# The softmax of q in the second to fourth block: two of its steps on GpSimd in place of VectorE

## Chip, cores and metric

The kernel runs on one core of a Trainium2 chip. The metric is the device time of one execution in microseconds (us), lower is better. The engines are named as in the profile: PE is TensorE's matrix products and PEld its weight loads, DVE is VectorE, ACT is ScalarE, POOL is GpSimd, SP is SyncE. A trailing q (SPq, DVEq) means an engine's sequencer.

## The reference

All in float32, cut to what matters:

```
# q, k, v: (4 batches, 8 heads, 576 tokens, 64)
q_s = softmax of q over its last axis (64 numbers of one token and head)
k_s = softmax of k over the tokens
kv  = k_s^T v                      # 64 x 64 for each batch and head
x   = q_s kv                       # -> 2304 tokens x 512
h   = x w1_in;  x = (h - tanh(h)) w1_out     # 512 -> 2048 -> 512
h   = x w2_in;  out = softplus(h) w2_out     # 512 -> 2048 -> 512
```

The softmax of q is q minus its maximum, the exponential, and a division by the sum plus 1e-9.

## The kernel before

The 2304 tokens are cut into five blocks of 512, 256, 512, 512 and 512 (SIZES; block index i counts from 0). For each block the attention output, transposed, is made by four tasks `x_task` (one for each pair of heads, hp), and the keys and values of a batch become the 128 x 128 matrices kv by four tasks `kv_task`. The first perceptron then runs in 16 steps over slices of its hidden layer: `hidden` makes h (L364), `gate` takes it through tanh on ScalarE, a subtraction on VectorE (L374, which reads h from PSUM), and a split into a high and a low part (L375 on ScalarE, L376 on VectorE), and `mid_out` (L391 to L393) multiplies by the second weight and adds up in PSUM. Each product is made of three, of high and low parts, to keep precision. Block sums go to memory, and the second perceptron runs over three spans of tokens with a scheme of seven products in place of eight (L459 onward); its last products are L529 to L531.

The weights need work first. They arrive as 64-bit numbers, and `convert` (L123 to L127, alternating between ScalarE and VectorE) makes them into 32-bit ones; `parts` (L132, L133) splits them. The second perceptron's input weights are added up in pairs (L212 to L215), split (L225, L226) and written to memory as `forms` (L227) while the first perceptron runs on blocks with index 2 and 3. All loads and stores stand in SyncE's queue: weights (L104, L109), k and v (L247), q (L311), forms.

An `x_task` has five stages with a pause between them: load q (L311); maximum over 64 columns (L320), subtraction (L322), exponential on ScalarE (L323); sum (L326), plus 1e-9 (L327), reciprocal (L328), normalisation into qn (L330); four transposes on PE (L339) and a copy (L341); product with kv (L346) and a split (L348, L349). The tasks of block i + 1 are started in the steps 1, 4, 8 and 10 of block i, and the `kv_task`s of the next batch in steps 0, 3, 6 and 9. These tasks have one buffer for each tile (q, qn, k, v and so on), so a load of q waits until the qn of the task before is made, and a qn waits for the transposes of the one before. The first block's tasks are interleaved by hand in a string (`order`) and have four buffers.

In a `kv_task`, GpSimd sets the extra columns of the tile v to 1 (L264), VectorE takes a maximum over the tokens of a partition (L268 to L270, tile m), PE transposes it (pm, L273), VectorE reduces it (L275), PE sends it back (pb, L278), VectorE subtracts it, reading it from PSUM (L280), ScalarE takes the exponential (L281), and PE multiplies with v (pk, L285). The normalised result goes into kv on ScalarE (L291).

The order of instructions on each engine is settled when the program is built: a scheduler goes through them by priority (the order in which they are written) and by its own estimate of when each is ready. On the chip each engine then runs its list in order.

The two steps in question run on the engine `eng`, which is GpSimd for the first block and VectorE for the others.

Of the kernel before, what the change touches and what calls it, by code (L numbers as in the profile page):

```python
# [19 lines left out]
def linear_attention_two_mlps(  # L20
# [28 lines left out]
    nc = tc.nc  # L49
# [5 lines left out]
    NB = len(SIZES)  # L55
# [25 lines left out]
    def psum_a(name):  # L81

        tag = wide.pop() if wide else "a"
        return ps.tile([P, 512], F32, tag=tag, name=name, bufs={"acc": 4, "a": 2}.get(tag, 1))
# [4 lines left out]
    def f32(ap):  # L89
        return ap.bitcast(F32)  # L90
# [209 lines left out]
    def x_task(i, hp, pool, bufs):  # L300

        nm = f"{i}_{hp}"
        n, J = SIZES[i], JS[i]
        qt = pool.tile([P, 2, J, D], F32, tag="q", name=f"q{nm}", bufs=bufs)
        segs = []
        r0 = 0
        while r0 < n:
            b, s = divmod(BASE[i] + r0, S)
            rows = min(n - r0, S - s)
            segs.append((b, slice(r0 // J, (r0 + rows) // J)))  # L310
            nc.sync.dma_start(  # L311
                out=qt[r0 // J : (r0 + rows) // J].rearrange("p h j d -> p h (j d)"),
                in_=q[b, 2 * hp : 2 * hp + 2, s : s + rows].rearrange("h (p j) d -> p h (j d)", j=J),
            )
            r0 += rows
        yield
        G = 2 * J
        qg = qt.rearrange("p h j d -> p (h j) d")
        mx = pool.tile([P, G], F32, tag="qm", name=f"qm{nm}", bufs=bufs)
        nc.vector.tensor_reduce(mx, qg, axis=AX, op=ALU.max)  # L320
        eng = nc.vector if i > 0 else nc.gpsimd
        eng.tensor_tensor(qg, qg, mx.unsqueeze(2).to_broadcast([P, G, D]), op=ALU.subtract)  # L322
        nc.scalar.activation(qt, qt, AF.Exp)  # L323
        yield
        sm = pool.tile([P, G], F32, tag="qsum", name=f"qsum{nm}", bufs=bufs)
        nc.vector.tensor_reduce(sm, qg, axis=AX, op=ALU.add)  # L326
        nc.vector.tensor_scalar(sm, sm, 1e-9, None, op0=ALU.add)  # L327
        nc.vector.reciprocal(sm, sm)  # L328
        qn = pool.tile([P, J, 2, D], F32, tag="qn", name=f"qn{nm}", bufs=bufs)
        eng.tensor_tensor(  # L330
            qn.rearrange("p j h d -> p h j d"),
            qt,
            sm.rearrange("p (h j) -> p h j", h=2).unsqueeze(3).to_broadcast([P, 2, J, D]),
            op=ALU.mult,
        )
        yield
        pt = psum_a(f"pt{nm}")
        for j in range(J):
            nc.tensor.transpose(pt[:, j * P : (j + 1) * P], qn[:, j].rearrange("p h d -> p (h d)"), ident)  # L339
        qs = pool.tile([P, n], F32, tag="qs", name=f"qs{nm}", bufs=bufs)  # L340
        nc.scalar.copy(qs, pt[:, :n])  # L341
        yield
        px = psum_a(f"px{nm}")
        pv, qv = (t.rearrange("p (j t) -> p j t", j=J) for t in (px[:, :n], qs))
        for b, c in segs:
            nc.tensor.matmul(pv[:, :, c], kv[b % 2, hp], qv[:, :, c], start=True, stop=True)  # L346
        xh, xl = (t[:, hp, :n] for t in xt[i])
        nc.scalar.activation(xh, px[:, :n], AF.Copy, scale=1.0 / WS)  # L348
        nc.vector.scalar_tensor_tensor(xl, px[:, :n], 1.0 / WS, f32(xh), op0=ALU.mult, op1=ALU.subtract)  # L349
# [216 lines left out]
    for i in range(NB - 1):  # L566
        for hp in range(NHP):
            if i < B - 1:
                at(i, KV_AT[hp], lambda i=i, hp=hp: kv_task(i + 1, hp, att, 1))
            at(i, X_AT[hp], lambda i=i, hp=hp: x_task(i + 1, hp, att, 1))  # L570
# [13 lines left out]
    wide += ["h0", "acc", "a", "acc", "h1", "acc", "a", "acc"] * 2 + ["h0", "acc", "a", "acc"]  # L584
    tasks = {f"k{hp}": kv_task(0, hp, pro, NHP) for hp in range(NHP)}
    tasks |= {f"x{hp}": x_task(0, hp, pro, NHP) for hp in range(NHP)}
    tasks["w"] = w_task(0)
    order = """k0 k1 k2 k3 x0 x1 x2 x3 k0 k0 k1 k1 w k2 k3 k2 k3 x1 k0 x0 k1 k0 x0 w x2 k2 x2 x3 x1 x3 k3 k1 x0 k2 x1 k3 x2 x3 x0 w x2 x3 w x1"""
# [13 lines left out]
    for n in range(min(starts), NB * NF - 2):  # L602
# [6 lines left out]
        while n >= -2 and len(gated) < min(n + 3, len(steps)):  # L609
            i, f = steps[len(gated)]  # L610
            gate(i, f, hidden(i, f, len(gated)))
            gated.append((i, f))
        if n >= 0:
            i, f = steps[n]
# [112 lines left out]
```

## Time and profile before

| | |
|---|---|
| median of 3 runs | 862.87 us (861.86 to 865.49) |
| the profiled execution | 860.99 us, of which 859.2 us lie between its first and last instruction (the span) |
| PE busy | 833.6 us, 97% of the span |
| DVE busy | 537.8 us, 63% |
| ACT busy | 409.3 us, 48% |
| POOL busy | 26.5 us, 3% (44 instructions) |
| chain that ended last | PE 83%, DVE 5%, ACT 5%, DMA 5%, issue 1% |
| mean granted TensorE clock | 0.996 of full speed |

Times in the trace count from the first instruction. A busy share is an average over stages with different limits: VectorE is at nine tenths or more in the first quarter of the span and far lower after it. PE counts as busy while a product is in its pipeline, so a busy PE is not a PE at its peak.

### The profile page before, as it was taken

How to read it: one execution, taken by the hardware profiler on the slowest of the kernel's cores; microseconds unless marked ns; L12 is line 12 of the kernel's file. 1: busy time of each engine (PE TensorE's matmuls, PEld its weight loads, DVE VectorE, ACT ScalarE, POOL GpSimd, SP SyncE). 2: the span in 40 equal slices, each digit the busy share in tenths (PEclk: the TensorE clock that was granted, in tenths of full speed). 3: DMA queues.
4: the chain of work that ended last, by engine and by line, in shares of the span. 5: the costliest groups of instructions: out<-in, count | busy, mean ns of one | idle time of the engine just before them, and what ended most of it. 6: DMA issues, size and time to landing. Idle time of an engine off the chain costs nothing.

```text
span 859.2 us, 11330 instructions
## 1 busy us (share of the span) xinstructions
PE 833.6 (97%) x4152; PEld 718.4 (84%) x4152; DVE 537.8 (63%) x926; ACT 409.3 (48%) x677; POOL 26.5 (3%) x44
## 2 busy tenths in 40 slices
PE   4899999999999999999999999999999999999997
PEld 4578789998787888878888889898899898998996
DVE  7899999998887534334797543357643454634433
ACT  4888666665655323223675442344432343423322
POOL 4000000000000000001011000001000010000000
PEclk9999999999999999999999999999999999999999
DMA  9798117667765010003544644446644444544411
GB/s 261 241 280 276 35 35 235 189 205 234 234 224 175 13 50 12 13 2 122 183 162 157 196 116 121 119 111 198 189 118 121 112 121 119 188 123 112 120 51 74
DMA packets 98616, 121.33 MB, mean 141 GB/s; under 512 B 38657, under 2 KB 62977, under 8 KB 98561
## 3 DMA queue, kind: packets, MB, share of 16 engines
q1 hardware_dynamic: 98560, 120.61, 46.4%
q8 instruction: 33, 0.54, 0.3%
q14 instruction: 23, 0.18, 0.1%
HBM read 96.47 MB, written 24.12 MB: 140 GB/s over the span
## 4 chain that ended last, share of the span: by engine, by line
PE 83%; DVE 5%; ACT 5%; DMA 5%; issue 1%; SPq 0%; ACTq 0%; DVEq 0%
PE h L364 18%; PE one L459 11%; PE o L530 8%; PE o L531 8%; PE o L529 8%; PE x L391 6%; PE x L393 6%; PE x L392 6%; PE seven L459 6%; PE two L459 3%; DMA rawi<-in_moe_w_in_dram 2%; PE px L346 2%; PE pk L285 1%; DMA forms<-stage 1%; DMA rawo<-in_moe_w_out_dram 1%
## 5 line engine op out<-in xcount | busy, mean ns | idle before, releaser
L364 PE MATMUL h<-xh,i 128*128 128x512 f32 (+1 forms) x640 | 202.2, 379 | 1.3 <-DVE i L133 0.7
L364 PEld LDWEIGHTS h<-xh,i 128*128 128x128 f32 x640 | 117.9, 189 | 24.3 <-DVE i L133 1.7
L364 PE MATMUL h<-xl,i 128*128 128x512 f32 (+1 forms) x320 | 118.8, 371 | 0.0
L392 PE MATMUL x<-gl,o 128*128 128x512 f32 (+1 forms) x320 | 118.6, 371 | 0.0
L393 PE MATMUL x<-gh,o 128*128 128x512 f32 (+1 forms) x320 | 118.4, 370 | 0.0
L459 PE MATMUL one<-xf,wf 128*128 128x384 f32 x576 | 116.7, 337 | 0.1
L391 PE MATMUL x<-gh,o 128*128 128x512 f32 (+1 forms) x320 | 116.2, 372 | 0.5 <-ACT gh L375 0.5
L530 PE MATMUL o<-o,gh 128*128 128x512 f32 x288 | 113.7, 395 | 0.0
L531 PE MATMUL o<-o,gh 128*128 128x512 f32 x288 | 113.7, 395 | 0.0
L529 PE MATMUL o<-o,gl 128*128 128x512 f32 x288 | 112.3, 390 | 0.0
L459 PEld LDWEIGHTS one<-xf,wf 128*128 128x128 f32 x576 | 103.0, 188 | 6.6 <-ACT u L474 0.4
L474 ACT COPY u<-one 128x384 f32<-128x384 f32 x72 | 34.5, 479 | 108.0 <-PE one L459 108.0
L374 DVE TENSOR_TENSOR g<-h,g 128x512 f32<-128x512 f32 (+1 forms) x80 | 50.5, 632 | 54.2 <-ACT g L373 54.0
L373 ACT ACTIVATE g<-h 128x512 f32<-128x512 f32 (+1 forms) x80 | 44.4, 555 | 82.1 <-PE h L364 81.7
L479 DVE TENSOR_TENSOR hh<-seven,u 128x384 f32<-128x384 f32 x48 | 26.6, 554 | 85.9 <-ACT u L474 85.9
L364 PEld LDWEIGHTS h<-xl,i 128*128 128x128 f32 x320 | 60.7, 190 | 10.8 <-issue 1.4
L391 PEld LDWEIGHTS x<-gh,o 128*128 128x128 f32 x320 | 60.6, 190 | 10.8 <-ACT gh L375 0.9
L392 PEld LDWEIGHTS x<-gl,o 128*128 128x128 f32 x320 | 60.3, 188 | 10.1 <-DVE gl L376 0.3
L393 PEld LDWEIGHTS x<-gh,o 128*128 128x128 f32 x320 | 60.3, 189 | 9.6
L375 ACT CAST gh<-g 128x512 fp32r<-128x512 f32 (+1 forms) x80 | 46.4, 580 | 36.8 <-DVE g L374 36.5
L531 PEld LDWEIGHTS o<-o,gh 128*128 128x128 f32 x288 | 54.0, 187 | 11.8
L376 DVE TENSOR_TENSOR gl<-g,gh 128x512 fp32r<-128x512 f32 (+1 forms) x80 | 50.9, 637 | 16.4 <-ACT gh L375 15.8
(95 smaller groups left out, 1188.3 us busy)
## 6 DMA issues: line engine op xcount, KB each, us to landing
wf<-forms SPq DMA_DIRECT2D x168, 256.0 KB, 2.7
rawi<-in_moe_w_in_dram SPq DMA_DIRECT2D x32, 512.0 KB, 5.6
rawo<-in_moe_w_out_dram SPq DMA_DIRECT2D x32, 512.0 KB, 5.1
forms<-stage SPq DMA_DIRECT2D x24, 512.0 KB, 3.5
v<-in_v_dram SPq DMA_DIRECT2D x32, 144.0 KB, 3.8
out_dram<-ot SPq DMA_DIRECT2D x18, 256.0 KB, 3.4
x2d<-x2s SPq DMA_DIRECT2D x16, 256.0 KB, 2.5
k<-in_k_dram SPq DMA_DIRECT2D x24, 144.0 KB, 3.3
```

The source lines that it names most:

```text
L364: nc.tensor.matmul(p, w[:, c], x[:, c, :n], start=at == 0, stop=at == 3 * NC - 1)
L373: tanh[0] = nc.scalar.activation(g, h, AF.Tanh)
L374: nc.vector.tensor_tensor(g, h, g, op=ALU.subtract)
L375: nc.scalar.copy(gh, g)
L376: nc.vector.tensor_tensor(gl, g, f32(gh), op=ALU.subtract)
L391: nc.tensor.matmul(a, ol[:, s], gh, start=first, stop=False)
L392: nc.tensor.matmul(a, oh[:, s], gl, start=False, stop=False)
L393: nc.tensor.matmul(a, oh[:, s], gh, start=False, stop=last)
L459: nc.tensor.matmul(a, w[:, wp, c], x[:, xp, c], start=first and at == 0, stop=at == 5, skip_group_check=True)
L529: nc.tensor.matmul(a, gl[:, c], oh, start=first, stop=False)
L530: nc.tensor.matmul(a, gh[:, c], ol, start=False, stop=False)
L531: nc.tensor.matmul(a, gh[:, c], oh, start=False, stop=last)
```

## The change

The condition that picks `eng` is turned round. Before, GpSimd served i = 0 alone; now VectorE serves the last block (i = 4) alone, and GpSimd serves i = 0 to 3. For i = 1, 2 and 3 (columns: 256, 512, 512) the subtraction of the maximum (L322) and the normalisation (L330) move from VectorE to GpSimd, for four pairs of heads each. Nothing else is edited.

```diff
@@ -318,7 +318,7 @@
         qg = qt.rearrange("p h j d -> p (h j) d")
         mx = pool.tile([P, G], F32, tag="qm", name=f"qm{nm}", bufs=bufs)
         nc.vector.tensor_reduce(mx, qg, axis=AX, op=ALU.max)
-        eng = nc.vector if i > 0 else nc.gpsimd
+        eng = nc.vector if i == NB - 1 else nc.gpsimd
         eng.tensor_tensor(qg, qg, mx.unsqueeze(2).to_broadcast([P, G, D]), op=ALU.subtract)
         nc.scalar.activation(qt, qt, AF.Exp)
         yield
```

## Rows read from the trace of the kernel before

**Rows 1.** Windows: busy us (x instructions) of PE, PEld, DVE, ACT, POOL; clock; DMA.

```profile
60.00:100.00 40.00, 38.29 (x178) 30.36 (x177) 38.51 (x65) 30.87 (x46) 0.22 (x2) 0.96 0.62 193
100.00:200.00 100.00, 99.75 (x674) 90.92 (x673) 94.94 (x217) 61.68 (x124) 0.65 (x6) 1.00 0.52 156
200.00:275.00 75.00, 71.84 (x344) 58.87 (x343) 63.42 (x133) 45.02 (x82) 0.32 (x3) 1.00 0.70 223
```

**Rows 2.** Waits of PE from 60 to 275 us: total, times, longest.

```profile
PE pm L273 <- DVE m L270: 3.4, 3, 1.6
```

**Rows 3.** Chain that ended last, 175 to 285: start, us, what.

```profile
193.90 0.70 DVE qn L330
194.65 0.34 SPq L311
...
196.48 6.64 DMA rawi<-in_moe_w_in_dram
...
272.44 0.60 DVE qn L330
```

**Rows 4.** DVE groups by form, 60 to 275: busy, mean ns, idle before.

```profile
L322 DVE TENSOR_TENSOR q<-q,qm 128x512 f32<-128x512 f32 x8 | 5.5, 685 | 0.1
...
L322 DVE TENSOR_TENSOR q<-q,qm 128x256 f32<-128x256 f32 x4 | 1.7, 416 | 0.0
```

**Rows 5.** Timeline of DVE, 432 to 437: start, us, instruction.

```profile
432.43 0.95 DVE L425 TENSOR_TENSOR xf<-xs,xf 128x768 fp32r<-128x768 f32 x1
...
434.17 0.68 DVE L374 TENSOR_TENSOR g<-h,g 128x512 f32<-128x512 f32 x1
434.77 2.02 DVE L425 TENSOR_TENSOR xf<-xs,xf 128x768 fp32r<-128x768 f32 x1
```

**Rows 6.** Timeline of DVE, 159 to 172.

```profile
164.30 0.68 DVE L322 TENSOR_TENSOR q<-q,qm 128x512 f32<-128x512 f32 x1
...
168.06 0.42 DVE L376 TENSOR_TENSOR gl<-g,gh 128x256 fp32r<-128x256 f32 x1
168.40 0.68 DVE L330 TENSOR_TENSOR qn<-q,qsum 128x512 f32<-128x512 f32 x1
```

**Rows 7.** POOL groups by form, whole span.

```profile
L330 POOL TENSOR_TENSOR qn<-q,qsum 128x512 f32<-128x512 f32 x4 | 4.4, 1130 | 0.1
L322 POOL TENSOR_TENSOR q<-q,qm 128x512 f32<-128x512 f32 x4 | 4.2, 1043 | 9.4 <-DVE qm L320 8.4 <-DVE qsum L327 1.0
```

**Rows 8.** Timeline of POOL.

```profile
165.19 0.11 POOL L264 MEMSET v<- 96x12 f32 x1 [12.24 <-PE pk L285]
...
433.52 2.44 POOL L446 TENSOR_TENSOR xs<-xs,t 128x768 f32<-128x768 f32 x1 [37.61 <-DVE xf L425]
```

**Rows 9.** DVE groups of all forms, 60 to 275.

```profile
L374 DVE TENSOR_TENSOR g<-h,g 128x512 f32<-128x512 f32 (+1 forms) x41 | 23.7, 578 | 2.9 <-ACT g L373 2.8
...
L280 DVE TENSOR_TENSOR k<-k,pb 96x768 f32<-96x768 f32 x11 | 10.4, 943 | 0.0
...
L326 DVE TENSOR_REDUCE qsum<-q 128x8 f32<-128x512 f32 (+1 forms) x12 | 7.0, 587 | 0.1
...
L349 DVE SCALAR_TENSOR_TENSOR xl<-px,xh 128x512 fp32r<-128x512 f32 (+1 forms) x10 | 5.8, 579 | 0.7 <-ACT xh L348 0.7
...
L275 DVE TENSOR_REDUCE mx<-pm 128x1 f32<-128x96 f32 x12 | 3.0, 250 | 0.9 <-PE pm L273 0.9
```

**Rows 10.** Windows of L322 alone: busy us (x) of DVE, of POOL.

```profile
60.00:100.00 40.00, 0.83 (x2) 0.00 (x0) 0.96 0.62 193
100.00:200.00 100.00, 4.25 (x7) 0.00 (x0) 1.00 0.52 156
200.00:275.00 75.00, 2.07 (x3) 0.00 (x0) 1.00 0.70 223
```

**Rows 11.** Timeline of PE, 172 to 180.

```profile
173.07 0.28 PE L392 MATMUL x<-gl,o 128*128 128x256 f32 x1
...
178.60 0.60 PE L339 MATMUL pt<-ident,qn 128*128 128x128 f32 x4
```

## Prediction

> **What bounds the kernel now.** I read the page first (its figures stand in the table above): TensorE is busy for nearly the whole span, and the chain that ended last is mostly TensorE. Late in the span it is a closed row of matrix products, so a change to the softmax can act only through stalls in the stretch where that softmax runs. I then cut that stretch into windows [rows 1]. The reader should look at the columns of PE and DVE. From 60 to 100 us both engines are nearly full (PE 38.29, DVE 38.51 of 40). From 100 to 200 PE is full (99.75) while DVE has 5.1 us of its 100 free (100.00 - 94.94). From 200 to 275 PE lacks 3.2 us (75.00 - 71.84). All that PE lacks in these three windows is 1.7 + 0.3 + 3.2 = 5.2 us, and that is nearly everything a faster softmax could win. The list of waits says what most of it is: the in-order PE stands at the transpose pm of the next key block until DVE has made the maximum m, 3.4 us in three waits [rows 2].
>
> The chain of work shows why the softmax matters there [rows 3]. At 272.44 the normalisation qn stands in DVE's queue directly before the last step of m, for which pm waits. At 193.90 qn is on the chain in another way: the next load of q waits for it in SyncE's queue (194.65), weight loads queue behind that, and the DMA of weights that the chain then waits for begins at 196.48 and takes 6.64 us.
>
> **What the change removes.** For block indices 1, 2 and 3, four head pairs each, two DVE instructions go: 24 in all. By the rows by form, 16 of them are of 512 columns at 0.685 us and 8 of 256 at 0.416 us [rows 4]. (The rows of L330 in that view repeat those of L322.) What DVE's queue gains is the distance between two starts, which is shorter than a duration: 0.60 us for 512 columns (434.17 to 434.77 [rows 5]) and 0.34 for 256 (168.06 to 168.40 [rows 6]). That is 16 x 0.60 + 8 x 0.34 = 12.3 us.
>
> **What it adds.** GpSimd needs 1.043 us for the subtraction and 1.130 on average for the normalisation at 512 columns [rows 7]; the second mean holds one instruction that was itself delayed, so I take 1.04. GpSimd at 256 columns isn't in the trace. Bounds: half of 1.04, which is 0.52, and all of it, 1.04. DVE's own ratio 0.416/0.685 gives 0.63, the nearest row, and I take that.
>
> A page of the Trainium skill sees the exchange worse: GPSIMD Engine Reference, section 3.1 (elementwise), measures an add of two tensors at 4497 against 2293 ns, a ratio of 1.96. The rows here give 1.04/0.685 = 1.52; here one operand is a broadcast of one number per 64, and no run shows whether that is the difference. By the page's ratio an instruction would take 1.34 us as an estimate, and the sum below would be about 5 us worse on DVE; the row decides, since it is this very instruction.
>
> **The price that no duration shows: DVE and GpSimd get in each other's way.** While GpSimd ran a subtraction from 433.52 for 2.44 us [rows 8], DVE's L374, which reads one operand from PSUM, kept its 0.68 us [rows 5]. The next one, L425 at 434.77, reads both operands from SBUF. It took 2.02 us instead of 0.95 [rows 5]: it ended 0.83 us after GpSimd did, about one instruction of its own. So a DVE instruction with two SBUF operands, started beside a GpSimd one, stands until that is done.
>
> How often will that happen? In 60 to 275 us DVE is busy for 196.9 us (the three DVE figures of [rows 1] added). Kinds that read PSUM or reduce, and so don't stand, are six groups with 23.7 + 10.4 + 7.0 + 7.0 + 5.8 + 3.0 = 56.9 us (the two reductions of the softmax have one row each with the same 7.0, of which one is shown) [rows 9]. The 24 instructions that go are 16 x 0.685 + 8 x 0.416 = 14.3. The rest, 125.7 of 182.6 us, is 69%, nearly all weight conversion and splitting; I count its plain copies among those that stand too. At 69% to meet one that stands at once, and 31% to run a free one first and then meet one, a 512-column instruction holds DVE for 0.69 x 1.04 + 0.31 x 0.69 x (1.04 - 0.60) = 0.81 us, one of 256 for 0.69 x 0.63 + 0.31 x 0.69 x (0.63 - 0.34) = 0.50. Sum: 16 x 0.81 + 8 x 0.50 = 17.0 us held against 12.3 saved, a **net of +4.7 us on DVE**. The bounds: never held, -12.3; held for the whole of each, 16 x 1.04 + 8 x 0.63 = 21.7, so +9.4.
>
> **What of that lies on the path.** The view of L322 by windows counts 2, 7 and 3 instructions in the three stretches [rows 10]; L330 has the same counts, so 4, 14 and 6 move. With +0.21 us for each of 512 columns and +0.16 for each of 256:
> 60 to 100 us holds four of the 256s, +0.6. Both engines are full there and the weight conversions feed PE, so all of it counts: **+0.6**.
> 100 to 200 us holds 14 (four of 256, ten of 512), +2.7. DVE has 5.1 us free there, and PE uses a gate's result late: gl, made at 168.06, is read at 173.07; qn of 168.40 is transposed only at 178.60 [rows 6, 11]. The longer path of one softmax (0.36 us more at each of two places, and a wait for DVE's running instruction, up to 0.6 each) fits in that slack. If this cover were gone the 2.7 would count whole. I let a quarter through, for the places where pm follows m closely: **+0.7**.
> 200 to 275 us holds six, +1.3 by the rate. Here the two chains pull apart. The SyncE chain gets later: qn ends 0.36 to 1.0 us after its time of now, then q, then the weights; I take +0.7, the middle. At 272.44 the removal gives 0.60 back, and the holding of DVE in front of m costs about as much (0.81). With +0.0 there, the stage gives **+0.7**.
> The loads of q are the same in number and size and stay in SyncE's queue; only their wait moves from DVE to GpSimd.
>
> GpSimd's queue is the other one that the steps enter. It is empty but for 0.11 us memsets of v, each of which waits for a product on PE. One is at 165.19 [rows 8]; the subtraction now runs on DVE at 164.30 [rows 6], before it. If it were queued behind the memset, it would come about 1 us later; the 10 us until its transpose hide that. ScalarE's exponential waits for the subtraction and DVE's sum for the exponential; both are later by the same amount, and the slack named is theirs too.
>
> Sum: 0.6 + 0.7 + 0.7 = **+2.0 us**. The profiled execution took 860.99 us (its span 859.2); it becomes 863.0. It lies 1.9 below the median of the runs shown, 862.87, to which the same 2.0 are added: **864.9 us**.
>
> **The rivals.**
> *Hidden anyway.* The gates' slack and DVE's free time take everything, and only some tenths show: 862.0 to 863.4, centre 862.9. For it speaks that PE is full from 100 to 200 us; against it that three waits for m, and the stretch before 100 us, have no slack.
> *Faster.* The holding rarely happens because the instructions fall beside PSUM-reading ones, so DVE gets most of its 12.3 us. Then the three waits for m go (3.4) and about 1 us of the 1.7 that PE lacks before 100 us: 862.9 - 4.4 = 858.5. Rows against it: 69% of DVE's time there is of the kind that stands.
> *Slower, clearly.* The holding comes near its upper bound. Place: 100 to 200 us, where 14 of the 24 lie and DVE has 5.1 us free. With a net of +9.4, 14/24 or more of it lies there (the large ones, about 6.2); beyond 5.1 it decides, since the conversions that follow are then late at pm and at the weights, and the rest (3.2) falls where nothing hides it. Together with the +0.7 of SyncE's queue and the part at pm about 6.5: 869.4. For it: GpSimd also waits for DVE's running instruction and then takes its turn whole. By the Trainium skill's ratio of 1.96 (GPSIMD Engine Reference, section 3.1) this case would be the likely one.
> *The order is made anew.* The program's scheduler places instructions by its own estimates, so freeing DVE may move others. That can give 2 us either way and is inside the range.
>
> **How the numbers follow.** Forecast (+0.5 to +4.3): 0.47. Hidden (within half a us or a little better): 0.22. Slower by more than 4.3 us: 0.22. Faster by more: 0.09. Half a per cent, 4.3 us, is about what a measurement of this kernel can tell from no change. So faster 0.09, same 0.69, slower 0.22. The range reaches to 859.5, past the hidden case to the faster one's edge, and to 870.0, which takes in the slower one.
>
> **What the profile afterwards would show.** Steps right: GpSimd busy some 22 us longer, with 24 more instructions of about 1.04 and 0.6 us; DVE instructions with two SBUF operands of 1 to 1.7 us beside them, L374 unchanged; DVE's busy time in 60 to 275 us not 12 lower but equal or higher; PE's lack in that stretch 5.2 + 2. Wrong: DVE's busy time falls by 10 us or more (no holding); or GpSimd takes 1.3 us or more for each; or PE stands at pt for qn, which would mean that the slack of 10 us was the order's and not the data's; or the loads of the weights start several us later and PE lacks 10 us or more before 275.

## The result, and the profile after

The changed kernel takes 872.12 us (median of four runs, 871.25 to 873.75) against 862.39 for the kernel before on the same chip (four runs, 861.86 to 865.49). The ratio is 1.0113, 95% interval 1.0094 to 1.0133: slower by 9.7 us. The forecast was 864.9 with a range up to 870.0; the time lies above it.

The profiled execution took 873.75 us, its span 872.0; it is the slowest of its four, 1.6 us above their median. Its mean granted clock is 0.989, where the run of 871.25 us had 0.995 and the profiled one of before 0.996; that much of what this trace shows may be this execution's own. Two experiments below, old_order and old_order_b, have a profiled execution that was disturbed, and their traces are not used.

Busy times first, from the page of the changed kernel:

```profile
PE 838.1 (96%) x4152; PEld 721.3 (83%) x4152; DVE 533.6 (61%) x902; ACT 409.5 (47%) x677; POOL 58.3 (7%) x68
```

The 24 instructions went over (902 on DVE where there were 926, 68 on POOL where there were 44). DVE is busy 4.2 us less than before (537.8). POOL is busy 31.8 us more (26.5 before). ACT's work is unchanged. No engine has 9.7 us more to do. PE was busy 4.5 us longer with the same 4152 products (838.1 for 833.6) and stood 8.3 us more, together the 12.8 us by which this span is longer than the one of before (872.0 for 859.2).

The same three windows as in [rows 1], busy us of PE, PEld, DVE, ACT, POOL, then the granted clock, the DMA share and GB/s:

```profile
60.00:100.00 40.00, 36.07 (x162) 29.12 (x161) 35.13 (x56) 28.14 (x40) 8.57 (x6) 0.91 0.58 185
100.00:200.00 100.00, 93.26 (x606) 83.99 (x605) 89.94 (x190) 59.42 (x119) 15.39 (x17) 0.98 0.51 152
200.00:275.00 75.00, 72.41 (x366) 60.17 (x365) 62.08 (x131) 45.20 (x83) 7.99 (x10) 1.00 0.65 212
```

What PE lacks is 3.9 + 6.7 + 2.6 = 13.3 us, where it was 5.2. The loss lies between 60 and 200 us, most of it from 130 to 200, where PE lacks 4.9 us instead of 0.3. In the same windows DVE is *less* busy than before, 35.13 for 38.51 and 89.94 for 94.94. An engine that had become the bound would be fuller. PE, DVE and ACT all have more holes, so the engines wait for each other more.

The lists of waits say for what, from 60 to 290 us: engine, its line, what it waited for; total us, times, longest. First PE, to be held against [rows 2]:

```profile
PE pm L273 <- DVE m L270: 6.2, 6, 1.6
PE pt L339 <- POOL qn L330: 2.9, 2, 1.9
PE pk L285 <- ACT k L281: 2.9, 1, 2.9
```

The known wait for m has grown from 3.4 to 6.2 (in before no further one falls between 275 and 290); 3.5 us of it lie between 130 and 200 us, where before has 0.2. The wait at the transpose of q for GpSimd's normalisation is new. The third, pk, has to do with keys and not with q at all, and it is longer rather than new, for the list of before has ("issue": nothing that the profile shows):

```profile
PE pk L285 <- issue: 1.2, 1, 1.2
```

ScalarE, in the view of the changed kernel:

```profile
ACT g L373 <- PE h L364: 16.2, 13, 3.4
ACT q L323 <- POOL q L322: 14.3, 9, 3.7
```

In the trace of before the exponential L323 stood 4.0 us for the subtraction, in six waits, 1.3 at most. Now it stands 14.3 in nine. The line of before:

```profile
ACT q L323 <- DVE q L322: 4.0, 6, 1.3
```

**One stall followed through.** Timelines of the changed kernel from 82 to 93 us, start, duration, instruction, and in brackets how long the engine had stood and for what. GpSimd:

```profile
83.09 3.81 POOL L322 TENSOR_TENSOR q<-q,qm 128x256 f32<-128x256 f32 x1 [9.93 <-DVE qm L320]
```

VectorE:

```profile
82.56 0.40 DVE L320 TENSOR_REDUCE qm<-q 128x4 f32<-128x256 f32 x1
82.88 1.21 DVE L124 SCALAR_TENSOR_TENSOR rawi<-rawi 128x1024 uint32<-128x1024 uint32 x1
84.02 1.21 DVE L127 SCALAR_TENSOR_TENSOR rawo<-rawo 128x1024 uint32<-128x1024 uint32 x1
85.15 0.68 DVE L376 TENSOR_TENSOR gl<-g,gh 128x512 fp32r<-128x512 f32 x1
85.75 0.68 DVE L125 TENSOR_SCALAR rawi<-rawi 128x1024 f32<-128x1024 f32 x1
89.42 1.23 DVE L133 TENSOR_TENSOR o<-rawo,o 128x1024 fp32r<-128x1024 f32 x1 [2.98 <-ACT o L132]
```

ScalarE:

```profile
82.67 0.62 ACT L375 CAST gh<-g 128x512 fp32r<-128x512 f32 x1
86.94 0.42 ACT L323 ACTIVATE q<-q 128x256 f32<-128x256 f32 x1 [3.65 <-POOL q L322]
87.26 0.58 ACT L373 ACTIVATE g<-h 128x512 f32<-128x512 f32 x1
87.74 0.65 ACT L123 ACTIVATE rawi<-rawi 128x512 uint32<-128x512 uint16 x1
88.29 1.10 ACT L132 CAST o<-rawo 128x1024 fp32r<-128x1024 f32 x1
...
91.91 0.84 ACT L281 ACTIVATE k<-k 96x768 f32<-96x768 f32 x1
```

TensorE:

```profile
89.50 0.39 PE L393 MATMUL x<-gh,o 128*128 128x512 f32 x1
92.80 2.97 PE L285 MATMUL pk<-v,k 96*128 96x130 f32 x12 [2.91 <-ACT k L281]
95.42 2.06 PE L391 MATMUL x<-gh,o 128*128 128x512 f32 x4
97.27 0.63 PE L364 MATMUL h<-xh,i 128*128 128x512 f32 x1
...
98.13 0.63 PE L339 MATMUL pt<-ident,qn 128*128 128x128 f32 x2
```

Read them downwards. The subtraction of 256 columns is issued when the maximum is ready and is finished only at 86.90. ScalarE's list has the exponential of this q next, so ScalarE stands 3.65 us. A tanh, a weight conversion and a weight's high part are queued behind it. VectorE's L133 then stands 2.98 us for that high part (L132), the keys' exponential comes at 91.91, and PE, whose list has pk next, stands 2.91 us. Behind that pause a product of 512 columns takes 0.63 us instead of 0.39. The granted clock is 1.00 from 80.0 to 89.8 us, before PE stood, and 0.50 from 92.8 to 97.0, behind the pause: 1.2 GHz, the lower of the two levels. Over 95 to 130 us it is 0.89, where before had 1.00 (the figure after PE, PEld, DVE, ACT and POOL):

```profile
95.00:130.00 35.00, 33.11 (x145) 27.00 (x145) 30.38 (x56) 19.95 (x34) 6.15 (x6) 0.89 0.19 43
```

One softmax step, whose q PE transposes at the earliest at 98.13, 15 us after the step was issued, has held up three engines through the *places* of other instructions in their lists. How much of the 9.7 us this one stall makes is another question: from 80 to 95 us PE is busy for 12.09 us here and was busy for 13.29 in before, which pauses there too (at a clock of 0.89). So it shows how the mechanism works; the pause is 1.2 us longer than before's, a small part of the loss.

### The profile page after: what moved, and what is told of

Read it like the earlier page. It is cut to its first block, busy times and chain, and to the rows that moved or that the text cites. A ratio compares the mean times of both kernels' runs of the same rounds, so it can differ in the third digit from the quotient of the medians.

```text
span 872.0 us, 11355 instructions
## 1 busy us (share of the span) xinstructions
PE 838.1 (96%) x4152; PEld 721.3 (83%) x4152; DVE 533.6 (61%) x902; ACT 409.5 (47%) x677; POOL 58.3 (7%) x68
## 4 chain that ended last, share of the span: by engine, by line
PE 73%; DVE 12%; ACT 5%; DMA 4%; issue 2%; POOL 2%; SPq 0%; POOLq 0%; ACTq 0%; DVEq 0%
PE h L364 14%; PE one L459 11%; PE o L530 8%; PE o L531 8%; PE o L529 7%; PE seven L459 6%; PE x L391 5%; PE x L393 5%; PE x L392 5%; PE two L459 3%; PE px L346 2%; DMA rawi<-in_moe_w_in_dram 1%; POOL q L322 1%; DVE stage L226 1%; DVE rawi L127 1%
## 5 line engine op out<-in xcount | busy, mean ns | idle before, releaser
L373 ACT ACTIVATE g<-h 128x512 f32<-128x512 f32 (+1 forms) x80 | 44.1, 551 | 74.7 <-PE h L364 74.4
L375 ACT CAST gh<-g 128x512 fp32r<-128x512 f32 (+1 forms) x80 | 46.1, 577 | 41.5 <-DVE g L374 41.4
L376 DVE TENSOR_TENSOR gl<-g,gh 128x512 fp32r<-128x512 f32 (+1 forms) x80 | 53.7, 672 | 17.7 <-ACT gh L375 17.2
```

Source lines behind the costliest of these rows:

```text
L373: tanh[0] = nc.scalar.activation(g, h, AF.Tanh)
L375: nc.scalar.copy(gh, g)
L376: nc.vector.tensor_tensor(gl, g, f32(gh), op=ALU.subtract)
```

## The experiments

Three theories were open. *Collision* (the expectations call it holding): GpSimd's time and its collisions with VectorE cost the 9.7 us directly, and any kernel with this work there pays. *Waiting*: the queues of other engines stand because GpSimd's results come later than VectorE's did. *Order*: the program's scheduler made new lists for every engine, and these place instructions so that the queues stand.

**Collision alone (spare_12).** The kernel before, to which GpSimd instructions of the same sizes are added for i = 1 and 2, writing a part of a tile that nobody reads (four more GpSimd instructions fill that part first). The lists of PE, DVE, ACT and SP are those of before.

```diff
+        if i in (1, 2):
+            c = J // 2
+            spare = xt[1][0][:, :c, 256:].rearrange("p c (g d) -> p c g d", d=D)
+            nc.gpsimd.tensor_tensor(spare, f32(spare),
+                mx.rearrange("p (c g) -> p c g", c=c).unsqueeze(3).to_broadcast([P, c, 4, D]),
+                op=ALU.subtract)      # and the same with qsum behind the normalisation
```

> The kernel before, with GpSimd instructions of the same sizes and operand kinds added for block indices 1 and 2, which start after the maximum and after the reciprocal but write a spare piece of SBUF that nobody reads; VectorE still does the real steps, and the lists of PE, DVE, ACT and SP are the same as before. Holding theory (DVE's two-operand instructions stand behind GpSimd, whoever needs the result): 8 x 0.50 + 8 x 0.81 = 10.5 us of DVE held with nothing saved, so 6 to 10 us slower, ratio 1.007 to 1.012. Waiting theory (queues stand for GpSimd's late result): nobody waits, ratio 0.999 to 1.003. Order theory (the build's new lists): lists unchanged, ratio 1.000.

Measured: 864.78 us, ratio 1.0021 (1.0004 to 1.0039). The collisions are there: timeline of VectorE in this kernel, the same instruction twice, the second beside a GpSimd instruction, whose row follows:

```profile
174.95 0.41 DVE L386 TENSOR_TENSOR gl<-g,gh 128x256 fp32r<-128x256 f32 x1
...
178.41 1.24 DVE L386 TENSOR_TENSOR gl<-g,gh 128x256 fp32r<-128x256 f32 x1
```

```profile
178.28 1.09 POOL L326 TENSOR_TENSOR xh<-xh,qm 128x512 fp32r<-128x512 f32 x1 [6.87 <-DVE qm L320]
```

They cost 0.2% for 16 instructions, without VectorE being relieved of anything: VectorE is busy 6.1 us longer (543.9 against 537.8), and some 1.8 us of that show in the time. Collision as the main cause falls; it expected 0.7 to 1.2%.

**Which part of the change (only_12, sub_only, norm_only).** The fourth block back on VectorE; the subtraction alone moved; the normalisation alone moved. The edits, shortened, against the changed kernel:

```diff
-        eng = nc.vector if i == NB - 1 else nc.gpsimd
+        eng = nc.gpsimd if i < 3 else nc.vector        # only_12
...
-        eng.tensor_tensor(qn...
+        norm = nc.gpsimd if i == 0 else nc.vector      # sub_only; norm_only the other way round
+        norm.tensor_tensor(qn...
```

> The changed kernel with block index 3 put back on VectorE. PE's gaps grew mostly between 60 and 200 us, where indices 1 and 2 are worked, so all theories expect most of the loss: ratio 1.007 to 1.011. Beside the run with spare instructions it tells how much of this the holding alone makes.

> The subtraction alone on GpSimd for indices 1 to 3; the normalisation stays on VectorE. Waiting theory: ScalarE stands at the exponential for the subtraction (14.3 us in the changed kernel), so this carries most: 5 to 8 us slower, ratio 1.006 to 1.009. Holding theory: half of the GpSimd instructions, half of the loss: 4 to 6 us, ratio 1.004 to 1.007.

> The normalisation alone on GpSimd for indices 1 to 3. Waiting theory: only PE's transposes wait for it (2.9 us in two waits), 1 to 3 us slower, ratio 1.001 to 1.004. Holding theory: half of the loss, 4 to 6 us, ratio 1.004 to 1.007.

Measured: only_12 870.81 us, 1.0076 (1.0052 to 1.0099); sub_only 868.38, 1.0052 (1.0028 to 1.0077); norm_only 868.65, 1.0050 (1.0033 to 1.0067). The loss has no single seat. sub_only and norm_only by themselves fit what the collision theory expected (0.4 to 0.7%) and lie outside what the waiting theory did (0.6 to 0.9% and 0.1 to 0.4%), though their intervals reach into it; it is spare_12 that speaks against collision. only_12 moves the same 16 instructions that spare_12 doubles, and costs 0.76% where spare_12 costs 0.21%: what differs is that here others wait for the results, VectorE has 16 fewer, and the lists are new.

**The change with the old lists (old_order, old_order_b, old_order_c).** The changed kernel, with edges of issue order added when it is built, so that PE, ACT, SP, and DVE without the 24, keep the lists of the kernel before. The three are the same kernel. The edit, shortened (the lists themselves are left out):

```diff
+def in_old_order(tc):
+    for steps in OLD:                       # one list for each engine
+        for a, b in zip(numbers, numbers[1:]):
+            tc.add_manual_dep(b, a.name, edge, reason="old order")
```

> The changed kernel, with the lists of instructions of PE, ACT and SP kept as in the kernel before, and DVE's as before without the 24 that moved (edges of issue order alone). Order theory (the new lists are what costs): back to a ratio of 0.998 to 1.003. Waiting theory (ScalarE's exponential, and PE's transposes, stand in their queues for a late GpSimd result, with other work behind them): the places of these in the lists are now even earlier against GpSimd, so as slow as the changed kernel or slower, ratio 1.009 to 1.016. Holding theory: about what the spare instructions cost, corrected for what DVE no longer does, ratio 1.001 to 1.004.

> The kernel of old_order once more, for a profile of an execution that was not disturbed. All theories that are left: the ratio again within 0.998 to 1.003. If ScalarE still stands at the exponential for GpSimd for 5 us or more in it, such waits are not what costs; if it hardly stands, the old lists simply give GpSimd more time.

> The kernel of old_order a third time, for a profile of an undisturbed execution. The ratio again 0.999 to 1.004. Waits in it: if the places in the lists are what costs, ScalarE's standing at the exponential for GpSimd falls well below the 14.3 us of the changed kernel, and PE's gaps from 60 to 290 us stay within 4 us of the kernel before; if the lists only hide it, the waits are as large and PE's gaps are not.

Measured: 863.99 us, 1.0009 (0.9992 to 1.0026); 863.42, 1.0021 (1.0000 to 1.0041); 863.22, 1.0006 (0.9984 to 1.0028). The same 24 instructions on GpSimd, with their collisions and their consumers, cost 0.1 to 0.2%, hardly to be told from nothing. The waiting theory, which expected 0.9 to 1.6% here, falls. The windows of old_order_c:

```profile
60.00:100.00 40.00, 37.99 (x176) 30.04 (x174) 37.96 (x61) 30.53 (x46) 5.10 (x6) 0.96 0.62 194
100.00:200.00 100.00, 99.32 (x666) 90.02 (x665) 93.02 (x201) 60.78 (x122) 16.06 (x20) 1.00 0.51 152
200.00:275.00 75.00, 71.39 (x345) 58.61 (x343) 61.84 (x126) 46.23 (x83) 7.31 (x9) 1.00 0.71 226
```

PE lacks 2.0 + 0.7 + 3.6 = 6.3 us, nearly the 5.2 of [rows 1], and from 100 to 200 us it is full again. ScalarE's wait for the subtraction is back to 4.2 (here L375 is the exponential):

```profile
ACT q L375 <- POOL q L374: 4.2, 6, 1.3
```

**The new lists without GpSimd (new_order).** The kernel before, VectorE doing all the softmax, with the lists of the changed kernel on PE, ACT, SP and DVE; the 24 steps, which those lists don't hold, are placed on DVE by the scheduler.

> The kernel before (VectorE does all steps), with the lists of PE, ACT, SP and of DVE's other instructions as in the changed kernel; the 24 steps in question are placed on DVE by the build. Order theory: most of the loss without any GpSimd work, ratio 1.007 to 1.012. Waiting and holding theories: no loss beyond 1 to 2 us, ratio 0.998 to 1.003.

Measured: 869.98 us, 1.0066 (1.0037 to 1.0094). Its waits of ScalarE (L373 is the exponential here, L372 the subtraction on VectorE):

```profile
ACT q L373 <- DVE q L372: 14.3, 9, 3.3
```

The same 14.3 us in nine waits as in the changed kernel, with none of the 24 steps on GpSimd. So these waits come with the lists and don't need GpSimd's slowness. The stage that lost most comes back with the lists as well:

```profile
100.00:200.00 100.00, 93.00 (x616) 83.89 (x615) 90.98 (x206) 58.89 (x117) 0.64 (x6) 0.98 0.50 153
```

PE lacks 7.0 us, where the changed kernel lacks 6.7 and before 0.3. The time lies just under the 0.7 to 1.2% that the order theory expected. The size is no clean price of the order, since these lists were made for a VectorE without the 24.

**One place alone (exp_late).** The changed kernel, with the exponential of blocks 1 to 3 put behind the next step's first tanh.

```diff
+        with tc.issue_after(tanh[0].ins):
+            nc.scalar.activation(qt, qt, AF.Exp)
```

> The changed kernel with the exponential of indices 1 to 3 issued one step later, behind the tanh of the step before on ScalarE. Waiting theory: ScalarE's waits at the exponential for GpSimd (14.3 us) fall to under 3 us and the loss to about what the normalisation alone makes, ratio 1.004 to 1.007. Holding theory: no change, ratio 1.010 to 1.012. Order theory: another order again, anything from 1.003 to 1.015, without regard to ScalarE's waits.

Measured: 873.68 us, 1.0105 (1.0067 to 1.0144): nothing gained. ScalarE's wait fell only to 7.0 us in six, where under 3 was expected, and the loss did not follow it. A single edge gives yet another set of lists, so this is no test of the exponential's place alone. That place isn't the one seat of the loss, for norm_only, where no exponential waits for a moved subtraction, loses 0.50%.

**One list alone (mix_pe).** The changed kernel with PE's list of before, and the lists of the change on the other engines.

> The changed kernel with PE's list as in the kernel before, and the lists of DVE, ACT and SP as in the changed one. If PE's list is at fault (transposes and key products put where their inputs are not ready): ratio 1.000 to 1.005. If the lists of DVE and ACT are at fault (the inputs come late whatever PE's list is): 1.008 to 1.014.

Measured: 876.69 us, 1.0178 (1.0143 to 1.0213), worse than either whole and outside both expectations. Lists of these two plans don't fit together, so this doesn't say what PE's list is worth.

**Lists from a plan with a slower GpSimd (slow_plan, slow_plan4, before_plan).** The lists are those that the scheduler makes when each of the 24 GpSimd steps stands twice, or four times, in the program; the kernel that runs has each step once. before_plan is the control: the kernel before, with lists made with its 24 steps twice on VectorE. In outline, the program from which the lists were taken (the kernel that runs has, as in old_order, only edges added):

```diff
+        for _ in range(2 if 0 < i < NB - 1 else 1):    # while the lists are made; 4 in slow_plan4
             eng.tensor_tensor(qg, qg, ..., op=ALU.subtract)
```

> The changed kernel, with the lists that the build makes when each of the 24 GpSimd steps stands twice in the program (the second copies are then left out). If the build takes GpSimd's steps for too short: GpSimd's result comes in time, ratio 1.002 to 1.007. If any list other than that of the kernel before costs about this much: 1.006 to 1.014.

> As slow_plan, with the lists that the build makes when each of the 24 GpSimd steps stands four times in the program. If too short an estimate of GpSimd's steps costs: less loss again than with twice, ratio 0.999 to 1.005. If the loss sits in DVE time that the lists count as free: as with twice, 1.005 to 1.009.

> The kernel before, with the lists that the build makes when each of the 24 steps stands twice on VectorE (the second copies are then left out), so lists with 12 us of DVE time to spare. If lists that plan too little DVE time are what costs: as the kernel before or faster, ratio 0.995 to 1.001. If the lists of before are just a favourable draw: slower, 1.003 to 1.010.

Measured: slow_plan 868.34 us, 1.0069 (1.0042 to 1.0095); slow_plan4 862.85, 1.0003 (0.9982 to 1.0024); before_plan 862.03, 1.0005 (0.9982 to 1.0027). With the step planned once, twice and four times, the change costs 1.13, 0.69 and 0.03%. slow_plan by itself fits both of its expectations; slow_plan4 fits only the one by which GpSimd's steps were planned too short. The control shows that other lists aren't dear in themselves: they differ from those of before in hundreds of places and cost nothing.

The page and the windows of slow_plan4, beside those of the changed kernel:

```profile
PE 834.0 (97%) x4152; PEld 718.2 (84%) x4152; DVE 534.4 (62%) x902; ACT 409.7 (48%) x677; POOL 57.9 (7%) x68
```

```profile
60.00:100.00 40.00, 37.56 (x174) 30.09 (x174) 36.55 (x59) 30.21 (x44) 8.57 (x6) 0.96 0.60 193
100.00:200.00 100.00, 96.72 (x647) 87.03 (x646) 93.49 (x205) 63.28 (x126) 15.44 (x19) 1.00 0.55 169
200.00:275.00 75.00, 74.79 (x364) 61.82 (x364) 63.01 (x128) 44.28 (x80) 8.68 (x10) 1.00 0.65 210
```

DVE and POOL do the same work in the same time as in the changed kernel (534.4 and 57.9 us; 533.6 and 58.3), collisions included. PE lacks 2.4 + 3.3 + 0.2 = 5.9 us instead of 13.3, and the kernel is 9 us faster. Even the slow subtraction of 3.81 us stands in it; around it only ScalarE's list has changed, with its exponential two instructions further back (timelines of POOL, then of ACT, in slow_plan4):

```profile
80.13 3.81 POOL L373 TENSOR_TENSOR q<-q,qm 128x256 f32<-128x256 f32 x1 [8.84 <-DVE qm L371]
```

```profile
80.49 0.59 ACT L424 ACTIVATE g<-h 128x512 f32<-128x512 f32 x1
80.98 0.69 ACT L174 ACTIVATE rawi<-rawi 128x512 uint32<-128x512 uint16 x1
83.97 0.42 ACT L374 ACTIVATE q<-q 128x256 f32<-128x256 f32 x1 [2.31 <-POOL q L373]
...
87.95 0.84 ACT L332 ACTIVATE k<-k 96x768 f32<-96x768 f32 x1
```

A tanh and a conversion run while the subtraction does, ScalarE stands 2.31 us instead of 3.65, and the keys' exponential starts 7.82 us after the subtraction instead of 8.82. Over the whole stretch its waits for the subtraction are 3.6 us in two:

```profile
ACT q L374 <- POOL q L373: 3.6, 2, 2.3
```

No version beats the kernel before: with good lists the 24 instructions are worth nothing either way.

## Why the prediction was wrong

**The step that failed** is the rival "The order is made anew", to which the prediction gave "2 us either way" and put inside the range. It is the case. With the old lists the change costs 0.1 to 0.2% (0.5 to 1.8 us), with lists of a plan that allows GpSimd more time nothing, and with the lists that it brings 1.13% (9.7 us); GpSimd and VectorE do the same instructions in all three (busy 53.7 to 58.3 and 533.6 to 534.7 us). So the lists make some 8 to 9 us, where 2 were allowed. The prediction costed the path through the lists of before as if they stayed. For that path its sum of +2.0 us came near, but partly by luck, since two of its terms, GpSimd's time and the holding of VectorE, were off in opposite directions (below).

**A cover that was named wrongly.** "The slack named is theirs too", it said of the exponential. The slack of qn belongs to the data of q. The exponential stands in ScalarE's one list, and the tanh and the weight conversions behind it had none there: the 3.65 us above went on to VectorE and PE. The prediction had the sign for it: PE standing at pt for qn "would mean that the slack of 10 us was the order's and not the data's". PE stood there, 2.9 us in two waits.

**Removed: right.** 24 instructions went from VectorE, worth 12.3 us by its sum.

**Added, GpSimd's time: half right.** Undisturbed, an instruction of 512 columns took 1.04 and one of 256 took 0.61, where 1.04 and 0.63 were estimated (timeline of POOL):

```profile
135.56 0.61 POOL L330 TENSOR_TENSOR qn<-q,qsum 128x256 f32<-128x256 f32 x1 [6.18 <-DVE qsum L328]
...
163.18 1.04 POOL L330 TENSOR_TENSOR qn<-q,qsum 128x512 f32<-128x512 f32 x1 [0.41 <-issue]
```

The means by form are longer (busy us, mean ns of one, idle before):

```profile
L322 POOL TENSOR_TENSOR q<-q,qm 128x512 f32<-128x512 f32 x12 | 13.7, 1139 | 75.8 <-DVE qm L320 74.8 <-DVE qsum L327 1.0
L330 POOL TENSOR_TENSOR qn<-q,qsum 128x512 f32<-128x512 f32 x12 | 13.5, 1134 | 17.5 <-DVE qsum L328 7.9 <-issue 6.3 <-ACT qs L341 2.4
L322 POOL TENSOR_TENSOR q<-q,qm 128x256 f32<-128x256 f32 x4 | 8.1, 2014 | 73.3 <-DVE qm L320 73.3
...
L330 POOL TENSOR_TENSOR qn<-q,qsum 128x256 f32<-128x256 f32 x4 | 5.3, 1335 | 13.1 <-DVE qsum L328 11.8 <-ACT rawo L123 1.4
```

The 256 columns took 1.3 to 2.0 us on average, so the upper bound, "all of it, 1.04", was no bound. For GpSimd's standing behind VectorE the prediction allowed up to 0.6 us each time; 3.81 for 0.61 is 3.2. GpSimd's busy time rose by 31.8 us, not 22. One of the prediction's signs of being wrong, "1.3 us or more for each", thus came true for 256 columns alone.

**Held: the mechanism is there, its size was off.** I compared each VectorE instruction from 60 to 290 us with the median of its line and form; ten are longer by more than 0.1 us, 6.7 us together, where 17.0 were forecast. So VectorE comes out at about -12.3 + 6.7 = -5.6 us (its busy time fell by 4.2 over the span; more than half of the 9.7 by which it fell from 60 to 275 us is work pushed behind 275), where +4.7 was forecast. The error lay mostly in the 69%: with it, about nine in ten of the 24 were to hold VectorE, and ten did, for 0.67 us each on average. From 83.09 on, as an example, it is GpSimd that stands, and VectorE loses nothing. The same count gives 8.6 us in 15 instructions in old_order_c and 8.2 us in 16 in slow_plan4: more holding than in the changed kernel, and little or no loss. The rival "Slower, clearly" came near the measured time (869.4) by a mechanism that did not occur: VectorE was not fuller from 100 to 200 us but emptier.

**By stage.** +0.6, +0.7 and +0.7 us were forecast for the three windows; PE's lack changed by +2.2, +6.5 and -0.6. The 100 to 200 us stage, which was to be covered best, paid most, since the cover was VectorE's free time and what was lost was the lists' agreement. The third term, SyncE's queue, is there as a path: the chain of the changed kernel goes from qn straight to the load of q.

```profile
204.73 1.06 POOL qn L330
...
205.80 2.32 DMA q<-in_q_dram
```

Its +0.7 us doesn't show in that window, where PE lacks 0.6 less than before.

**What stays open.** Whether the scheduler's estimate lacks GpSimd's own duration or its standing beside VectorE: the estimate itself was not read, and the three plans show an effect in the expected order and no more. Which places of which list cost how much: the waits for m from 130 to 200 us, in which the largest part of the loss shows, were not followed back, and exp_late and mix_pe show that single places or lists can't be exchanged by themselves.

## What to carry to other kernels

Where a scheduler builds the queues, moving an instruction to another engine is two changes: the work that moves, and new lists for everybody. Cost the second by a test of its own, the new kernel with the old lists, before the instruction is blamed. And for every moved producer look up which in-order queue holds its consumer and what stands behind it there: the slack to count is that of the whole queue, not of the one value.

## What was not expected of the hardware

GpSimd and VectorE stand for each other in both directions, and a waiting GpSimd can be passed over more than once. Its subtraction of 256 columns, 0.61 us of work when alone (at 121.45 us in old_order_c), was open from 83.09 to 86.90, while VectorE ran four instructions one behind another, without a gap, from 82.88 to 86.43. The same 3.81 us stand in only_12, sub_only, slow_plan and slow_plan4. VectorE's 1.24 us for its usual 0.41 (spare_12) is the other side. The Trainium skill, SBUF — State Buffer, section "SBUF: two separate sides", describes the port pair that the two engines share as an exclusive lock between a GpSimd instruction and, for one, a VectorE instruction with two SBUF inputs: whoever starts first has it for the whole instruction, and the other is blocked. Both rows agree with that; the row of 3.81 us reads as if the lock can go to several VectorE instructions in a row before GpSimd gets it. For all that, the collisions were cheap: 0.2% for 16 GpSimd instructions between 60 and 200 us, where VectorE of before is busy for more than nine tenths [rows 1].
